# Deviations turned by a small product, and another order of the last five pairs, in a spectral filter with a softmax-gated feed-forward

## The chip, the cores and the metric

The kernel runs on one core of a Trainium2 chip. The core has a matrix engine (TensorE), a vector engine (VectorE, DVE in the profile), a scalar engine (ScalarE, ACT), a general engine (GpSimd, POOL), and a queue engine that only issues transfers (SyncE, SP). Each has its own instruction stream, carried out in order; semaphores tie the streams together. ScalarE and POOL issue transfers too. Products land in PSUM[...].

The metric is the device time of one execution in microseconds. The kernel before took 1626.26 us, the median of three runs (1624.71 to 1630.68).

## The reference

```python
X = np.fft.rfft(x, axis=1)                     # x: (8, 3136, 256)
Y = X * (filt_r + 1j * filt_i)[None]
x = np.fft.irfft(Y, n=3136, axis=1).reshape(25088, 256)
h = x @ w_in                                   # (25088, 1024)
e = np.exp(h - h.max(-1, keepdims=True))
solu = h * e / (e.sum(-1, keepdims=True) + 1e-9)
mu = solu.mean(-1, keepdims=True)
var = ((solu - mu) ** 2).mean(-1, keepdims=True)
out = ((solu - mu) / np.sqrt(var + 1e-6) * g_ln) @ w_out      # (25088, 256)
```

Everything is float32 (the filters and weights come as given to the kernel). Of the deviations this document speaks of, there is one for each of the 25088 rows: 1/sqrt(var + 1e-6). The kernel folds the mean and g_ln into w_out, so that a row of the result is its row of solu times the folded weights, times that row's deviation.

## The kernel before, in words

**Two halves that run together.** The Fourier filter of the eight batch elements is a sequence of small matrix products with trips through DRAM in between (tiles d1 and d2). Element 0 is filtered in a start-up phase. The others are filtered while the feed-forward works on earlier elements. `PLAN` says at which step each piece of an element's filter runs: its first products (`first_at`, line L269 for elements from 2 on), its spectrum (`spectrum_at`, L301 forward and back), and its way back to rows (`back_at`, L372). The filtered rows lie transposed in the tile `y`, which holds two elements.

**The feed-forward's steps.** The 25088 rows are 196 blocks of 128. Two blocks are a pair for the first product; four blocks are a group. `step(k)` is called for k from 0 to 204 (196 blocks and a lag of 9), and writes out by hand what each engine gets, in this order; there is no planner beyond it. `j` is k // 2. With `hid` (k below 196) the step runs products of x with w_in, and with `proj` it runs products with w_out of a pair p that is four to five pairs behind: an odd step has products 1, 2, 6, 7 of p = j - 4, the even step after it products 5, 3, 4 of the same p.

**Seven products in place of eight.** Both matrix products are done by halves in Winograd's form: four sums of quarters of the left operand (`pair_sums`, `project_sums`, on POOL, line L702), sums of weights made once, and seven half-size products (`product`, L723, 128x512 each; `project`, L844, four times 128x128 each). In PSUM the seven go to two banks for the output product (`o0`, `o1`) and two or three for the first (`m0`, `m1`). Products 1, 6, 5 and 3 of a pair all go to bank 0, on top of each other, and ScalarE takes the value out in between: after product 1, after 6 and after 5 (`keep_out`, L856, a scaled copy by the row's deviation), and after 3. Products 2, 7 and 4 go to bank 1, and VectorE joins each with what ScalarE has kept (`finish_out`, L860). `store_out` (L868) sends the pair's 256 rows to DRAM on SP's queue.

**From solu to the left operand of the second product.** `exponential` (L755, ScalarE), `normalize` (L766 to L771, VectorE), `turn` (L787, a 32x32 block transpose on VectorE into a tile `turn` for the group), `square` (L779, ScalarE: the variance of each row, four columns for a group's four blocks). `regroup(p, i)` (L799) then moves quarters of the turned group into tiles `solu_t` in eight DMAs of 128 KB for a pair, on SP's queue. Each quarter takes rows from all four blocks of the group, so the rows of a pair in the second product are not those of two blocks, and a pair's regrouping can only start when all four blocks of its group have been turned. `project_sums(p, 0)` and `project_sums(p, 1)` make the four sums from these tiles in two places of the pair's even step.

**Deviations.** `deviations` (L806 to L810), in the even step in which a group's first pair is regrouped, computes the 128x4 deviations on POOL and stores them to a DRAM row. `regroup_deviations` (L816), one step later, reads them back in the regrouped order with four DMAs:

```python
rows = rs_rows.pop(g).rearrange("(a p) b -> b p a", p=32)
for b in range(4):
    dma(out=rss[g][32 * b:32 * b + 32, :], in_=rows[b])
```

The DMA queue is SP's, but POOL's for the last group. The tile `rs_t` that they fill is what `keep_out` and `finish_out` scale by. In SP's order an even step has: eight regroupings, the deviations' store, two output stores, then loads for the filter; the odd step has the deviations' four reads.

**The first spectrum fetch of an element** (`fetch`, L291) reads d1, which POOL's stores (L280) have just filled. It is issued on ScalarE's queue, except for a part of element 1. Element 2's first one is issued at the end of step 14.

**The tail.** Steps 196 to 204 have no first products any more: TensorE has only the products of the last pairs, 93 to 97. Pair 97 is regrouped one even step after pair 96, though both belong to group 48.

Of the kernel before, what the change touches and what calls it, by code (L numbers as in the profile page):

```python
# [17 lines left out]
P = 128  # L18
# [76 lines left out]
def kernel(  # L95
# [14 lines left out]
    wi_dram = nc.inline_tensor(wi_host, name="wi_tbl").ap()  # L110
    wb_dram = nc.inline_tensor(wb_host, name="wb_tbl").ap()
    de_dram = nc.inline_tensor(de_host, name="de_tbl").ap()

    def pool(name, bufs, space=None, stack=ctx):
        kw = {} if space is None else {"space": space}
        return stack.enter_context(tc.tile_pool(name=name, bufs=bufs, **kw))
# [67 lines left out]
    class Spectrum:  # L184
# [114 lines left out]
        def product(self, i, out, lhsT, rhs):  # L299
            for v in range(self.units[i][1]):  # L300
                nc.tensor.matmul(out=out[:, v, :], lhsT=lhsT(v), rhs=rhs[:, v, :],  # L301
                                 start=True, stop=True)
# [311 lines left out]
    def psum_pair(name, other):  # L614
# [7 lines left out]
    hpool = pool("hp", 2)  # L622
    wk = pool("wk", 1)
    spool = pool("sp", 1)
    rs_dram = pool("rs_dram", 2, DRAM)
    pools |= {name: pool(name + "1", bufs)
             for name, bufs in (("r", 4), ("diff", 1), ("t2", 1), ("p", 1), ("g", 1))}
    pools["de"] = pool("de1", 2)
    second.pools = pools
    for c, at, n, kind, dims in (  # L630
            (0, 0, 4 * C, "t2", "p (v c) -> p v c"), (0, 4 * C, 4 * C, "f", "p (v k c) -> p v k c"),
# [48 lines left out]
    def load_de(sp, u):  # L680
# [3 lines left out]
                            in_=de_dram[i:i + pairs].rearrange("i p k u q -> p i (k u q)"))  # L684
        return de

    turns, variances, solu_ts, solu_sums, rs_rows, rss, pos, ots = (
        {} for _ in range(8))
    sums, ms, hs, nmaxs, es, solus, squares = {}, {}, {}, {}, {}, {}, {}


# [9 lines left out]
    def sum_of(out, in0, in1, op):  # L701
        nc.gpsimd.tensor_tensor(out=out, in0=in0, in1=in1, op=op)  # L702

    def pair_sums(j):

        s14 = upool.tile([P, 2, P], FP32, name=f"s14_{j}", tag="s14")
        s23 = wk.tile([P, 2, P], FP32, name=f"s23_{j}", tag="s23")
        sums[j] = s1, s2, s3, s4 = s14[:, 0, :], s23[:, 0, :], s23[:, 1, :], s14[:, 1, :]
        a11, a12, a21, a22 = (tokens(2 * j + i, c) for i in range(2) for c in range(KD))
        sum_of(s1, a21, a22, ALU.add)  # L710
        sum_of(s2, s1, a11, ALU.subtract)
        sum_of(s3, a11, a21, ALU.subtract)
        sum_of(s4, a12, s2, ALU.subtract)
# [76 lines left out]
    def regroup(p, i):  # L790


        g, second = divmod(p, 2)
        turned = turns[g].rearrange("p (k q) b i -> p k q (b i)", q=4)
        a = 2 * second + i
        st = upool.tile([P, KF, P], FP32, name=f"solu_t_{p}_{i}", tag=f"solu_t{i}")
        solu_ts[p, i] = st[:, 0:KF // 2, :], st[:, KF // 2:KF, :]
        for q in range(4):
            nc.sync.dma_start(out=st[32 * q:32 * q + 32, :, :],  # L799
                              in_=turned[32 * a:32 * a + 32, :, q, :])  # L800

    def deviations(p, dma):
        g, second = divmod(p, 2)
        if not second:
            rs = small.tile([P, 4], FP32, name=f"rs_{g}", tag="rs", bufs=2)
            nc.gpsimd.tensor_scalar(out=rs, in0=variances.pop(g), scalar1=1.0 / DFF, scalar2=EPS_LN,  # L806
                                    op0=ALU.mult, op1=ALU.add)
            nc.gpsimd.tensor_tensor(out=rs, in0=rs, in1=neg_half, op=ALU.pow)
            rs_rows[g] = rows = rs_dram.tile([P, 4], FP32, name=f"rows_{g}", tag="rows")
            dma(out=rows, in_=rs)  # L810

    def regroup_deviations(g, dma):
        rows = rs_rows.pop(g).rearrange("(a p) b -> b p a", p=32)
        rss[g] = small.tile([P, 4], FP32, name=f"rs_t_{g}", tag="rs_t")
        for b in range(4):
            dma(out=rss[g][32 * b:32 * b + 32, :], in_=rows[b])  # L816

    def project_sums(p, step):

        (a11, a12), (a21, a22) = solu_ts[p, 0], solu_ts[p, 1]  # L820
        if step == 0:
            s1 = upool.tile([P, KF // 2, P], FP32, name=f"u1_{p}", tag="u1")
            sum_of(s1, a21, a22, ALU.add)
            sum_of(a21, a11, a21, ALU.subtract)
            solu_sums[p] = s1, None, a21, None
        else:
            s2 = spool.tile([P, KF // 2, P], FP32, name=f"u2_{p}", tag="u2")
            s4 = spool.tile([P, KF // 2, P], FP32, name=f"u4_{p}", tag="u4")
            s1, _, s3, _ = solu_sums[p]
            sum_of(s2, s1, a11, ALU.subtract)  # L830
            sum_of(s4, a12, s2, ALU.subtract)
            solu_sums[p] = s1, s2, s3, s4

    def project(p, m):

        bank = {1: 0, 6: 0, 5: 0, 3: 0, 2: 1, 7: 1, 4: 1}[m]
        if m in (1, 2):
            pos[p, bank] = ps_o.tile([P, DFF // 2], FP32, name=f"o{m}_{p}", tag=f"o{bank}")[:, 0:P]
        s1, s2, s3, s4 = solu_sums[p]
        lhs = {1: solu_ts[p, 0][0], 2: solu_ts[p, 0][1], 4: solu_ts[p, 1][1], 5: s1, 6: s2, 7: s3,  # L840
               3: s4}[m]
        w = w_out_sb[:, {1: 0, 2: 1, 3: 2, 5: 3, 6: 4, 7: 5, 4: 6}[m]]
        for f in range(KF // 2):
            nc.tensor.matmul(out=pos[p, bank], lhsT=lhs[:, f, :], rhs=w[:, f, :],  # L844
                             start=f == 0 and m in (1, 2, 7), stop=True, skip_group_check=True)

# [5 lines left out]
    def keep_out(p, i, to):  # L854
        rs = out_half(p, i, 0)[1]
        nc.scalar.activation(out=out_half(p, *to)[0], in_=pos[p, 0], func=AFT.Copy, scale=rs)  # L856
# [12 lines left out]
        del ots[p]  # L869

    blocks = NT * B // 2

# [8 lines left out]
    for e in range(1, B):  # L883
# [24 lines left out]
        for i, t in enumerate(spectrum_at):  # L908

            other = e == 1 and i % 2 == 1 and t + 1 < LAG  # L910


            dma = nc.sync.dma_start if e == 1 and t < 8 else nc.scalar.dma_start
            fetches = ahead(t, 2) if e == 1 and t < 8 or e == 2 and i == 0 else spectrum_loads[t - 2]
            fetches.append(lambda sp=sp, i=i, dma=dma: sp.fetch(i, dma))
            ahead(t, 1 if e == 1 and i % 2 == 1 else 2).append(lambda sp=sp, i=i: sp.fetch_filter(i))
            fetches.append(lambda sp=sp, i=i: sp.fetch_de(i))
            early[t].append(lambda sp=sp, i=i, o=other: sp.forward(i, psum_pair(f"pb_{sp.e}_{i}", o)))
            add = (nc.gpsimd if t + 1 < LAG else nc.vector).tensor_tensor
            first_parts[t].append(lambda sp=sp, i=i, add=add: sp.multiply(i, 0, add))  # L920
            (top if t + 1 < LAG else second_parts)[t + 1].append(
                lambda sp=sp, i=i, add=add: sp.multiply(i, 1, add))
            late[t + 1].append(lambda sp=sp, i=i, o=other: sp.inverse(i, psum_pair(f"pc_{sp.e}_{i}", o)))
            stores[t + 2].append(lambda sp=sp, i=i: sp.store(i, nc.gpsimd.dma_start))
# [23 lines left out]
    def step(k):  # L948
# [23 lines left out]
        if not odd:  # L972
# [4 lines left out]
                exponential(k - 2)  # L977
            if proj:
                project(p, 5)
                keep_out(p, 1, (0, 1))  # L980
            if blocks <= k < blocks + 2:
                exponential(k - 2)
            if hid and k > LAG:
# [2 lines left out]
                turn(k - 3)  # L986
            if hid and k > LAG:
                finish(j, k, 0, (k, 0), 1)
            if proj:
                finish_out(p, 1, 1, (0, 1), 1)  # L990
            for job in early[k]:
                job()
# [4 lines left out]
                keep(j, k + 1, 0)  # L997
            if proj:
                project(p, 3)
                keep_out(p, 0, (0, 1))  # L1000
                project(p, 4)
            for job in spectrum_loads[k]:
                job()
            if 0 <= j - 3 < pairs:
                regroup(j - 3, 0)
                regroup(j - 3, 1)
            if j - 3 == pairs - 2:
                deviations(j - 3, nc.gpsimd.dma_start)
            if 0 <= j - 4 < pairs:
                project_sums(j - 4, 1)  # L1010
            if j - 3 == pairs - 2:
                regroup_deviations((j - 3) // 2, nc.gpsimd.dma_start)
            elif 0 <= j - 3 < pairs:
                deviations(j - 3, nc.sync.dma_start)
            if hid:
                product(j, 7)
            if 2 <= k < blocks + 2:
                normalize(k - 2)
            for job in second_parts[k] + middle[k] + first_parts[k]:
                job()  # L1020
            if proj:
                finish_out(p, 1, 0, (1, 0), 1)
                store_out(p)
        else:
# [13 lines left out]
            if hid:  # L1038
                product(j, 3)
                product(j, 4)  # L1040
            if 0 <= j - 3 < pairs:
                if (j - 3) % 2 == 0 and j - 3 < pairs - 2:
                    regroup_deviations((j - 3) // 2, nc.sync.dma_start)
            if proj:
                project(p, 6)
                project(p, 7)
# [20 lines left out]

    with tc.manual_schedule():
        pair_sums(0)
        for load in first_loads:  # L1070
            load()
        for k in range(blocks + LAG):
            step(k)
# [30 lines left out]
```

## Time and profile before

| What | Value |
|---|---|
| Median of three runs | 1626.26 us |
| Profiled execution, its own time | 1619.98 us |
| Its span | 1618.2 us |
| TensorE's mean granted clock | 0.991 |
| TensorE busy (PE) | 1548.8 us, 96% |
| VectorE busy (DVE) | 1302.4 us, 80% |
| POOL busy | 1169.3 us, 72% |
| ScalarE busy (ACT) | 903.4 us, 56% |
| Second products, L844 | 402.1 us and 311.0 us |
| First products, L723 | 396.6 us and 308.0 us |
| DMA packets | 377245, of them 62762 under 512 B |

How to read it: the busy time of an engine is the time in which at least one of its instructions ran. PE is the matmuls, PEld the loads of weights, which run under matmuls. Every f32 product is recorded as two matmuls and two loads, so that four 128x128 products are a piece of eight records. A row of a timeline gives the start in us from the span's start, the duration, the engine and line, the tile written and those read, the shape and how many records were merged; in square brackets, the idle time before it and what ended it. A q after an engine's name (SPq, ACTq) is its queue of issued transfers.

### The profile page before, as it was taken

To read this page: it belongs to the slowest core of one execution; us is meant where nothing else is said; L and a number is where in the kernel's file an instruction comes from. 1 tells how busy PE (TensorE), PEld (TensorE's weight loads), DVE (VectorE), ACT (ScalarE), POOL (GpSimd) and SP (SyncE) were. 2 spreads that over 40 slices of the span, in tenths; PEclk is the share of its full clock that TensorE was granted. 3 is DMA by queue.
4 is the path that set the end of the run, shared out by engine and by line. 5 is a ranking of instruction groups with operands and counts; after the bars stand their busy time and mean duration, and the time that the engine had idled before them with its cause. 6 is when DMAs were issued, how large, how long until landed. Compare 5 with 4: busy or idle time off the path is not lost. (4 is left out here: it accounts for less than half of the span.)

```text
span 1618.2 us, 37006 instructions
## 1 busy us (share of the span) xinstructions
PE 1548.8 (96%) x12710; PEld 1048.2 (65%) x12710; DVE 1302.4 (80%) x2630; ACT 903.4 (56%) x1772; POOL 1169.3 (72%) x1333
## 2 busy tenths in 40 slices
PE   5899899999999999999999999999999999999997
PEld 1363456666766677667766676667676777777776
DVE  1686877998898989997999789897988777777772
ACT  2135555566565655666656655566556566665662
POOL 4446887579777877797688867788666766677775
PEclk8999999999999999999999999999999999999999
DMA  9888878877788778866887668866785454444443
GB/s 268 245 268 249 244 208 229 223 209 196 203 246 231 201 189 243 241 192 167 211 251 200 186 180 229 238 180 169 215 234 151 121 135 122 104 112 105 110 110 102
DMA packets 377245, 312.13 MB, mean 193 GB/s; under 512 B 62762, under 2 KB 342835, under 8 KB 377059
## 3 DMA queue, kind: packets, MB, share of 16 engines
q1 hardware_dynamic: 304340, 168.63, 40.3%
q0 software_dynamic: 34624, 101.68, 20.7%
q10 hardware_dynamic: 38096, 39.46, 8.1%
q8 instruction: 103, 1.69, 0.5%
q14 instruction: 82, 0.67, 0.1%
HBM read 124.86 MB, written 81.50 MB: 128 GB/s over the span
## 5 line engine op out<-in xcount | busy, mean ns | idle before, releaser
L844 PEld LDWEIGHTS o<-w_out_sb,solu_t 128*128 128x128 f32 x3136 | 382.8, 192 | 49.3 <-issue 43.9
L723 PE MATMUL m<-w_in_sb,s 128*128 128x512 f32 x784 | 396.6, 607 | 9.9 <-ACT h L733 9.2
L844 PE MATMUL o<-w_out_sb,solu_t 128*128 128x128 f32 x3136 | 402.1, 276 | 2.9 <-DVE ot L860 2.0
L844 PEld LDWEIGHTS o<-w_out_sb,u 128*128 128x128 f32 x2352 | 307.3, 192 | 144.4 <-issue 109.7
L844 PE MATMUL o<-w_out_sb,u 128*128 128x128 f32 x2352 | 311.0, 275 | 7.4 <-ACT ot L856 4.6
L723 PE MATMUL m<-w_in_sb,y 128*128 128x512 f32 x588 | 308.0, 607 | 4.8 <-DVE h L744 2.9
L771 DVE SCALAR_TENSOR_TENSOR h<-e,rsum,h 128x1024 f32<-128x1024 f32 x196 | 302.1, 1541 | 6.9
L733 ACT COPY h<-m 128x512 f32<-128x512 f32 x294 | 172.9, 588 | 237.0 <-PE m L723 204.2
L702 POOL TENSOR_TENSOR u<-solu_t 128x512 f32<-128x512 f32 x98 | 133.3, 1361 | 219.3 <-DMA solu_t<-turn 134.6
L856 ACT ACTIVATE ot<-o,rs_t 128x128 f32<-128x128 f32 x392 | 143.6, 366 | 258.3 <-PE o L844 241.2
L779 ACT ACTIVATE h<-h,nmu 128x1024 f32<-128x1024 f32 x196 | 224.9, 1148 | 53.2 <-DVE turn L787 43.0
L747 DVE CUSTOM_DVE_ANT_0 h<-m,h 128x512 f32<-128x512 f32 x196 | 134.1, 684 | 140.3 <-ACT h L733 102.6
L787 DVE STREAM_TRANSPOSE turn<-h 128x1024 f32<-128x1024 f32 x196 | 243.2, 1241 | 3.2
L755 ACT ACTIVATE e<-h,nmax 128x1024 f32<-128x1024 f32 x196 | 225.1, 1149 | 8.8 <-DVE h L771 8.4
L702 POOL TENSOR_TENSOR u<-solu_t,u 128x512 f32<-128x512 f32 x98 | 149.0, 1520 | 93.4 <-PE o L844 89.2
L723 PEld LDWEIGHTS m<-w_in_sb,s 128*128 128x128 f32 x784 | 128.6, 191 | 98.3 <-issue 85.0
L860 DVE SCALAR_TENSOR_TENSOR ot<-o,rs_t,ot 128x128 f32<-128x128 f32 x294 | 102.0, 347 | 77.0 <-ACT ot L856 60.6
L723 PEld LDWEIGHTS m<-w_in_sb,y 128*128 128x128 f32 x588 | 96.3, 191 | 102.1 <-issue 52.9
L702 POOL TENSOR_TENSOR u<-u,solu_t 128x512 f32<-128x512 f32 x98 | 161.6, 1649 | 0.9
L702 POOL TENSOR_TENSOR solu_t<-solu_t,solu_t 128x512 f32<-128x512 f32 x98 | 153.4, 1565 | 7.7
L702 POOL TENSOR_TENSOR s<-y 128x128 f32<-128x128 f32 x196 | 95.6, 488 | 0.5
L372 PEld LDWEIGHTS py<-wb_t,t 50*64 50x64 f32 x3584 | 57.6, 134 | 42.9 <-issue 22.5
(116 smaller groups left out, 1965.4 us busy)
## 6 DMA issues: line engine op xcount, KB each, us to landing
solu_t<-turn SPq DMA_DIRECT2D x784, 128.0 KB
out_dram<-ot SPq DMA_DIRECT2D x196, 128.0 KB
t<-d POOLq DMA_DIRECT2D x112, 200.0 KB, 6.0
d<-x POOLq DMA_DIRECT2D x100, 200.0 KB, 5.1
f<-f_dram POOLq DMA_DIRECT2D x39, 512.0 KB, 7.2
d<-g POOLq DMA_DIRECT2D x39, 512.0 KB, 4.8
t<-d ACTq DMA_DIRECT2D x37, 512.0 KB
x<-in_x_dram SPq DMA_DIRECT2D x112, 98.0 KB
```

The source lines that it names most:

```text
L372: nc.tensor.matmul(out=views[g][64 * h:64 * h + 64, cb, i, :], lhsT=t4[rows, i, c0:c0 + 64], rhs=wb_t[rows, 0:N1], start=True, stop=True)
L702: nc.gpsimd.tensor_tensor(out=out, in0=in0, in1=in1, op=op)
L723: nc.tensor.matmul(out=ms[j, bank], lhsT=lhsT, rhs=w_in_sb[:, w, :], start=m in (1, 2, 7), stop=True, skip_group_check=True)
L733: nc.scalar.copy(out=h_half(k, i), in_=ms[j, 0])
L747: nc.vector.tensor_tensor_reduce(out=h_half(k, i), in0=ms[j, bank], in1=h_half(*kept), scale=1.0, scalar=sofar, op0=ALU.add, op1=ALU.min, ...
L755: nc.scalar.activation(out=e, in_=hs[k], func=AFT.Exp, bias=nmaxs.pop(k)[:, 1:2], scale=-1.0, accum_out=esum)
L771: nc.vector.scalar_tensor_tensor(out=solu, in0=e, scalar=rsum, in1=solu, op0=ALU.mult, op1=ALU.mult, accum_out=nmu)
L779: nc.scalar.activation(out=solu, in_=solu, func=AFT.Square, bias=nmu, scale=-float(DFF), accum_out=variances[g][:, i:i + 1])
L787: nc.vector.transpose(out=turns[g][:, :, i, :], in_=solus[k].rearrange("p (f j) -> p f j", j=32))
L844: nc.tensor.matmul(out=pos[p, bank], lhsT=lhs[:, f, :], rhs=w[:, f, :], start=f == 0 and m in (1, 2, 7), stop=True, skip_group_check=True)
L856: nc.scalar.activation(out=out_half(p, *to)[0], in_=pos[p, 0], func=AFT.Copy, scale=rs)
L860: nc.vector.scalar_tensor_tensor(out=ot, in0=pos[p, bank], scalar=rs, in1=out_half(p, *kept)[0], op0=ALU.mult, op1=ALU.add)
```

## The change

**Deviations.** The trip through DRAM goes. A constant tile `turn_t` (128x36, loaded once on POOL's queue) holds a one at column (row modulo 32) in its first 32 columns and a one at column (row // 32) in its last four. POOL multiplies the first 32 columns by each of the group's four deviations into a tile of 128x128 (`wide`), in the same place where the deviations were stored. One even step later than `deviations`, behind product 4, TensorE multiplies that tile (as weights) with the last four columns of `turn_t`, and the 128x4 result is the regrouped deviations. It lands in four free columns of the bank that products 2, 7 and 4 of that step's pair use (`places`), and ScalarE copies it to `rs_t`. For the last group too, everything is done this way.

**Sums.** The first place makes sums 1 and 2, the second sums 3 and 4 (before: 1 and 3, then 2 and 4).

**Last five pairs** (`last`, pairs 93 to 97). Product 3 goes to a bank of its own, `m0`, free by then. After product 5 ScalarE takes bank 0 out twice, once for each half of the rows, and VectorE joins product 3 with the second copy in an instruction more. All joins and the store of such a pair come ahead of that step's other VectorE work. The last pair's regrouping follows that of the pair ahead of it in the same step, into a buffer of another pool.

**One fetch** of element 2, the first of its spectrum, moves from ScalarE's queue to SP's.

```diff
+    rows = np.arange(P)[:, None]
+    turn_dram = nc.inline_tensor(np.concatenate(
+        [rows % 32 == np.arange(32), rows // 32 == np.arange(4)], 1).astype(np.float32),
+        name="turn_tbl").ap()
...
-    def deviations(p, dma):
-        g, second = divmod(p, 2)
-        if not second:
...
-            rs_rows[g] = rows = rs_dram.tile([P, 4], FP32, name=f"rows_{g}", tag="rows")
-            dma(out=rows, in_=rs)
...
+    def deviations(g):
...
+        spreads[g] = wide = spread.tile([P, 4, 32], FP32, name=f"wide_{g}", tag="wide")
+        nc.gpsimd.tensor_tensor(
+            out=wide, in0=turn_t[:, 0:32].rearrange("p (o i) -> p o i", o=1).broadcast_to([P, 4, 32]),
+            in1=rs.rearrange("p (b o) -> p b o", o=1).broadcast_to([P, 4, 32]), op=ALU.mult)
+
+    def regroup_deviations(g, ps):
+
+        nc.tensor.matmul(out=ps, lhsT=spreads.pop(g).rearrange("p b i -> p (b i)"), rhs=turn_t[:, 32:36],
+                         start=True, stop=True)
         rss[g] = small.tile([P, 4], FP32, name=f"rs_t_{g}", tag="rs_t")
-        for b in range(4):
-            dma(out=rss[g][32 * b:32 * b + 32, :], in_=rows[b])
+        nc.scalar.copy(out=rss[g], in_=ps)
...
         if step == 0:
             s1 = upool.tile([P, KF // 2, P], FP32, name=f"u1_{p}", tag="u1")
+            s2 = spool.tile([P, KF // 2, P], FP32, name=f"u2_{p}", tag="u2")
             sum_of(s1, a21, a22, ALU.add)
+            sum_of(s2, s1, a11, ALU.subtract)
+            solu_sums[p] = s1, s2
+        else:
+            s4 = spool.tile([P, KF // 2, P], FP32, name=f"u4_{p}", tag="u4")
+            s1, s2 = solu_sums[p]
             sum_of(a21, a11, a21, ALU.subtract)
...
-        bank = {1: 0, 6: 0, 5: 0, 3: 0, 2: 1, 7: 1, 4: 1}[m]
+        alone = m == 3 and p in last
+        bank = 2 if alone else {1: 0, 6: 0, 5: 0, 3: 0, 2: 1, 7: 1, 4: 1}[m]
+        if alone:
+            pos[p, bank] = ps_m.tile([P, DFF // 2], FP32, name=f"o{m}_{p}", tag="m0")[:, 0:P]
...
+    last = range(blocks // 2 - (LAG + 1) // 2, blocks // 2)
...
-            dma = nc.sync.dma_start if e == 1 and t < 8 else nc.scalar.dma_start
+            dma = nc.sync.dma_start if e == 1 and t < 8 or e == 2 and i == 0 else nc.scalar.dma_start
...
             if proj:
                 project(p, 5)
-                keep_out(p, 1, (0, 1))
+                keep_out(p, 1, (1, 1) if p in last else (0, 1))
+            if p in last:
+                keep_out(p, 0, (0, 1))
+                finish_out(p, 1, 1, (1, 1), 1)
...
+            if j >= 4 and j % 2 == 0 and j - 4 < pairs:
+                regroup_deviations((j - 4) // 2, places.pop(p) if proj else psum("ps_rs")[:, 0, 0:4])
...
-            if 0 <= j - 3 < pairs:
-                regroup(j - 3, 0)
-                regroup(j - 3, 1)
-            if j - 3 == pairs - 2:
-                deviations(j - 3, nc.gpsimd.dma_start)
+            if 0 <= j - 3 < pairs - 1:
+                for n in range(j - 3, pairs if j - 3 == pairs - 2 else j - 2):
+                    regroup(n, 0)
+                    regroup(n, 1)
...
+            if 0 <= j - 3 < pairs and j % 2:
+                deviations((j - 3) // 2)
             if hid:
                 product(j, 7)
+            if p in last:
+                finish_out(p, 0, 1, (0, 1), 2)
+                finish_out(p, 1, 0, (1, 0), 1)
+                store_out(p)
...
-            if 0 <= j - 3 < pairs:
-                if (j - 3) % 2 == 0 and j - 3 < pairs - 2:
-                    regroup_deviations((j - 3) // 2, nc.sync.dma_start)
```

## The prediction

> **What bounds the kernel now.** I read the busy shares first, then what TensorE waited for, then busy time by stretch of the span, and last the timelines of the places where TensorE stood still. The page and its chain:
>
> ```profile
> span 1618.2 us, 37006 instructions
> PE 1548.8 (96%) x12710; PEld 1048.2 (65%) x12710; DVE 1302.4 (80%) x2630; ACT 903.4 (56%) x1772; POOL 1169.3 (72%) x1333
> PE 42%; DMA 4%; DVE 1%; SPq 1%; issue 1%; ACT 0%; POOL 0%; DVEq 0%; POOLq 0%; ACTq 0%
> ```
>
> TensorE has 69.4 us without work in 1618.2; nearly all of the traced chain is its products. Two stretches (columns: PE, PEld, DVE, ACT, POOL, clock, DMA share, GB/s):
>
> ```profile
> 1300.00:1400.00 100.00, 100.00 (x915) 72.89 (x914) 76.21 (x168) 60.13 (x119) 67.32 (x79) 1.00 0.47 121
> 1580.00:1618.00 38.00, 26.42 (x216) 24.67 (x215) 7.98 (x18) 9.22 (x22) 19.97 (x19) 0.99 0.40 104
> ```
>
> In the middle TensorE is the bound: what is added to it is paid in full, and what is taken from other engines is worth only the stalls it ends. From 300 to 1300 these stretches leave 9.1 us idle in all, from 130 to 300 some 18 us, in the tail 11.6 us, half of it after the last product. TensorE's longest waits after the start-up (total, times, longest):
>
> ```profile
> PE m L723 <- ACT h L733: 9.2, 6, 3.4
> PE pa L269 <- POOL x L260: 5.5, 6, 2.6
> PE o L844 <- ACT ot L856: 4.6, 8, 1.0
> PE o L844 <- POOL u L702: 2.8, 2, 1.5
> ```
>
> [...] each f32 product is recorded as two loads and two matmuls, and in the one row where 128-column weights meet a shorter stream (98 columns) the pace is
>
> ```profile
> 91.50 14.43 PE L395 MATMUL py<-wi_t,t 100*128 100x98 f32 x128
> ```
>
> 14.43/128 = 0.113 us, hardly more than the 0.111 us of the 128-column stream (1.78 us for 16). So under a short stream the load sets the pace. [...] 62762 packets are under 512 B, and 49 groups with 512 four-byte elements and 128 rows, counted on two sides, are 62720.
>
> **The change, part by part.**
>
> *Small product, +11.0 us.* It has two 128-column loads and two matmuls of 4 columns. At 0.113 us a pair that is 0.226 us; 49 groups make 11.0 us, all on TensorE. The four columns hide no load: the second load and that of the next product lie bare. Bounds: if one of the loads still found cover, 0.113 us (5.5 us); if the pipeline drained around it, two loads of 0.192 us and a fill of 0.17 us (a product of 8 records lasts 1.06 us but follows at 0.89 us), 0.55 us (27 us). I take 0.226, because products of different tiles and banks follow each other in the trace without a gap. Its operand comes from POOL two steps (some 12 us) earlier, so it should not wait for it.
>
> *Work of POOL and ScalarE, +1.0 us.* The 128x4x32 multiplication is not in the trace; nearest is `s<-y` 128x128 at 0.488 us, so 49 times 23.9 us. POOL's idle time (it waits 134.6 us for regrouped tiles alone) covers it, except early, where TensorE waits for POOL's sums (0.94 us at 173.53, 0.97 at 215.41), each behind a deviation: 0.5 us each. Without cover anywhere it would be 23.9. The ScalarE copy, 0.2 to 0.36 us (accumulator read 0.19, a 128x256 copy 0.356), stands where ScalarE waits for the next product anyway. Behind it are DMA issues of the spectrum and, in the next step, the half that product 3 waits for; 2 us of products lie between. [...]
>
> *DMAs taken away, -2.5 us.* SP loses 240 issues (48 at 0.55, 192 at 0.42 us, near 107 us), POOL five, and with them the waits of SP for the row's landing (31.2 us). SP is not on the path by itself. What TensorE can get back are stalls beside these transfers: 2.36 us at 491.85 (ScalarE's own DMA issue stood still while SP put out the four row reads), 0.58 and 1.02 at 1047 and 1049 (a half waited for `rs_t`), 0.97 at 215.41. That is 4.9; I take half, since transfers of 80% share stay around them.
>
> *First fetch of batch element 2, from ScalarE's queue to SP's, -3.4 us.* ScalarE:
>
> ```profile
> 237.89 0.37 ACT L856 ACTIVATE ot<-o,rs_t 128x128 f32<-128x128 f32 x1
> 243.67 0.38 ACTq L291 DMA_DIRECT2D t<-d  x1
> 244.70 0.58 ACT L733 COPY h<-m 128x512 f32<-128x512 f32 x1 [6.44 <-issue]
> ```
>
> The fetch waits for stores that POOL issues until 239.83. Behind it stands the half that product 3 needs, and TensorE loses 3.36 us at 245.43. On SP it is queued behind two output stores, and ahead of the next row loads and regroupings; the forward product that needs it ran at 255.54, so 252 without the stall. Issued at 244 to 246 it should land by then. If it does not, up to 3 us return; I count the gain whole. Its table load remains with ScalarE, without that wait.
>
> *Order of the sums, 0.* POOL does the same four sums; product 6 now has its operand a sum (1.27 us) sooner, product 7 a sum later. Only the tail has such a wait.
>
> *Tail, -4.6 us.* Now:
>
> ```profile
> 1585.68 3.35 PE L844 MATMUL o<-w_out_sb,solu_t 128*128 128x128 f32 x24 [0.33 <-DVE ot L860]
> 1590.36 1.16 PE L844 MATMUL o<-w_out_sb,u 128*128 128x128 f32 x8 [1.33 <-POOL u L702]
> 1606.92 1.16 PE L844 MATMUL o<-w_out_sb,u 128*128 128x128 f32 x8 [1.52 <-POOL u L702]
> 1611.38 1.06 PE L844 MATMUL o<-w_out_sb,solu_t 128*128 128x128 f32 x8
> 1585.54 5.36 SPq L799 DMA_DIRECT2D solu_t<-turn  x8
> 1592.43 6.88 SPq L799 DMA_DIRECT2D solu_t<-turn  x8
> 1603.04 1.26 POOL L702 TENSOR_TENSOR u<-solu_t 128x512 f32<-128x512 f32 x1 [4.05 <-DMA solu_t<-turn]
> ```
>
> The 31 products from 1574.23 would end at 1602.0 without gaps (31 times 0.89 us and 0.17 us of pipeline), and end at 1612.4: 10.4 us of gaps. Not all go. Product 3 in its own bank no longer waits for the evacuation after product 5 (0.72 us a pair), but product 4 still needs VectorE's join of the first half, so some 0.2 us stays. More binding: the last turn ends at 1585.4, and VectorE and ScalarE bring it no sooner. Both regroupings issue from there: pair 96 to 1590.9, its tiles in by 1593.4, two sums of 1.3 us to 1596.1, product 6 then, the rest of the pair with POOL's third and fourth sums to 1601. Pair 97 issues to 1596.3 and lands near 1600 (3.7 us later, as now), two sums to 1602.6; product 6 at 1603.0, then four more at 0.9 us: end at 1607.8 for 1612.4. The joins and 5.8 us to the end stay. Bounds: nothing (the transfers share what they have) to 10.4.
>
> *Sum:* 11.0 + 1.0 - 2.5 - 3.4 - 4.6 = +1.5 us. The profiled execution's span goes from 1618.2 to 1619.7, and its own time from 1619.98 to 1621.5. The median of the runs, 1626.26, lies 6.3 us above that execution; I carry the difference over: 1627.8.
>
> **The rivals.** *A, slower:* the small product drains the pipeline, 0.55 us each, 27 us: +17.5, about 1644. Place: every second even step, behind product 4. It decides from (8.1 + 9.5)/49 = 0.36 us on. For it: one product alone shows 1.06 us against 0.89. Against it: changes of bank and weights cost nothing visible elsewhere. *B, faster:* timed runs are 6.3 us longer than the profiled one; if that is transfer stalls which leave with the small packets, and all 4.9 us of named stalls go too, the sum is 1.5 - 2.4 - 6.3 = -7.2, and with a tail that closes by 7 us -9.6: 1617 to 1619. Against it: from 1300 to 1570 there is no stall left to end. *C, the tail's gain does not come* because both regroupings share the transfer time: +6.1, 1632, still no change. *D, the moved fetch lands late:* +4.9, 1631.
>
> **How the numbers follow.** 0.5% is 8.1 us, about what a measurement of this kernel can tell from no change. Likeliest case 0.38, C 0.12 and D 0.10, all within it (0.60 less 0.02 for combined misses); A and milder forms of it 0.25; B 0.17 to below the bound. So faster 0.17, same 0.58, slower 0.25. The range reaches down into B to 1617 and up into A to 1640; the likeliest's own is 1621 to 1634.
>
> **What would show it.** Small products as a row with 98 matmuls, each group lengthening the stretch behind product 4 by 0.2 to 0.25 us; from 1300 to 1570 of now TensorE stays full and a period of four blocks (24.5 us) grows by that much. ScalarE without the 6.44 us at 244. No packets under 512 B to speak of. The last TensorE product some 4 to 5 us closer to the end of the last hidden product. The forecast is wrong if the small product's pace is over 0.36 us, or if new waits of TensorE for POOL's spread tile, VectorE or SP's queue appear.

## The result and the profile after

The kernel after took 1627.58 us, the median of 13 runs (1622.91 to 1630.88), beside 1626.26 us for 13 runs of the kernel before. The ratio is 0.9991, with an interval of 0.9972 to 1.0011: no difference. The forecast was 1627.8 us, and "no change" its likeliest case. The total is right, but it came from the wrong terms, as the experiments show: the term for the transfers was too small by 18 us, the moved fetch had the wrong sign, and the tail brought nothing.

The two profiled executions should not be set against each other as wholes. That of before ran in 1619.98 us and that of after in 1629.27 us: 9.3 us apart, where the medians differ by 1.3. So the traces are read here by stretch, and sizes are taken from the timed ratios (1% is 16.3 us).

The page of the kernel after:

```profile
span 1627.3 us, 37027 instructions
PE 1557.7 (96%) x12808; PEld 1060.1 (65%) x12808; DVE 1314.6 (81%) x2635; ACT 911.8 (56%) x1821; POOL 1193.7 (73%) x1378
DMA packets 342555, 311.93 MB, mean 192 GB/s; under 512 B 28058, under 2 KB 308147, under 8 KB 342371
```

TensorE has the 98 matmuls of the small products more, and 69.6 us without work, as before (69.4). The busy shares tell nothing of what happened. Of the packets under 512 B some 34,700 are gone and 28,058 are left, so the prediction was wrong to put all 62,762 down to the deviations. It counted each four-byte piece on two sides; an experiment below, with fewer pieces, shows it counted once.

The quiet middle and the tail (columns: PE, PEld, DVE, ACT, POOL, clock, DMA share, GB/s):

```profile
1300.00:1400.00 100.00, 100.00 (x973) 72.96 (x973) 78.89 (x172) 61.30 (x124) 66.91 (x77) 1.00 0.46 118
1589.00:1627.30 38.30, 24.71 (x194) 23.79 (x194) 7.59 (x19) 7.13 (x19) 16.76 (x15) 0.90 0.32 88
```

The middle is full, as before. The tail, which the change was to close up, has 13.6 us without work for TensorE where before had 11.6 in its last 38 us, and a clock of 0.90 for 0.99.

The small product in that middle (timeline of TensorE; start, duration), first before, then after:

```profile
1406.93 1.06 PE L844 MATMUL o<-w_out_sb,solu_t 128*128 128x128 f32 x8
1407.82 1.88 PE L723 MATMUL m<-w_in_sb,s 128*128 128x512 f32 x4
1409.54 1.72 PE L844 MATMUL o<-w_out_sb,solu_t 128*128 128x128 f32 x14
```

```profile
1411.15 1.06 PE L858 MATMUL o<-w_out_sb,solu_t 128*128 128x128 f32 x8
1412.05 0.28 PE L822 MATMUL o<-turn_t,wide 128*128 128x4 f32 x2
1412.19 1.96 PE L728 MATMUL m<-w_in_sb,s 128*128 128x512 f32 x4
1413.99 1.95 PE L858 MATMUL o<-w_out_sb,solu_t 128*128 128x128 f32 x16
```

From product 4 of the pair (L844, now L858) to the next output product TensorE takes 1413.99 - 1411.15 = 2.84 us. Before it took 1409.54 - 1406.93 = 2.61 us. Here the product is paid in full and not more: 0.23 us.

The first fetch of element 2, now on SP's queue, and what waited for it (timelines of SP and TensorE):

```profile
243.42 0.40 SPq L295 DMA_DIRECT2D t<-d  x1
252.06 0.32 PE L376 MATMUL py<-wb_t,t 50*64 50x49 f32 x4 [1.86 <-DMA t<-d]
253.29 1.35 PE L376 MATMUL py<-wb_t,t 50*64 50x49 f32 x60 [0.91 <-DMA t<-d]
258.51 2.01 PE L305 MATMUL pb<-t,de 64*64 64x256 f32 x16 [3.86 <-DMA t<-d]
```

ScalarE's wait of 6.44 us is gone, but TensorE now waits 3.86 us for the fetched tile itself, and 2.77 us for tiles of the way back in the same stretch. Its busy time from 200 to 250 us rose from 44.07 to 46.83 us, and from 250 to 300 us fell from 48.04 to 42.13 us, at a granted clock of 0.90 for 1.00.

The tail after (SP, ScalarE and TensorE):

```profile
1592.27 10.80 SPq L807 DMA_DIRECT2D solu_t<-turn  x16
1603.17 19.94 SPq L883 DMA_DIRECT2D out_dram<-ot  x8
1608.64 0.37 ACT L871 ACTIVATE ot<-o,rs_t 128x128 f32<-128x128 f32 x1 [9.61 <-DMA out_dram<-ot]
1609.15 2.05 PE L858 MATMUL o<-w_out_sb,u 128*128 128x128 f32 x8 [8.43 <-ACT ot L871]
1610.99 1.80 PE L858 MATMUL o<-w_out_sb,solu_t 128*128 128x128 f32 x8
1621.00 1.16 PE L858 MATMUL o<-w_out_sb,solu_t 128*128 128x128 f32 x8
```

The two pairs are regrouped together, in 16 issues of 10.8 us. The output store of pair 94 stands behind these 16 on SP's queue and starts at 1603.17. There are two output tiles `ot`, taken in turn, so pair 96 needs the one that pair 94 has not yet given back: ScalarE waits 9.61 us for the store, and TensorE 8.43 us for ScalarE. From the last product of x with w_in (the last hidden product) to the last product of all it is 43.2 us, counted between the starts of the last records of the two; before had 40.1.

### The profile page after: what moved, and what is told of

Same layout as the page of the kernel before. It is cut to its first block, busy times and chain, and to the rows that moved or that the text cites. A ratio compares the mean times of both kernels' runs of the same rounds, so it can differ in the third digit from the quotient of the medians.

```text
span 1627.3 us, 37027 instructions
## 1 busy us (share of the span) xinstructions
PE 1557.7 (96%) x12808; PEld 1060.1 (65%) x12808; DVE 1314.6 (81%) x2635; ACT 911.8 (56%) x1821; POOL 1193.7 (73%) x1378
## 2 busy tenths in 40 slices
DMA packets 342555, 311.93 MB, mean 192 GB/s; under 512 B 28058, under 2 KB 308147, under 8 KB 342371
## 4 chain that ended last, share of the span: by engine, by line
PE 72%; DMA 8%; DVE 2%; issue 1%; SPq 1%; POOL 1%; ACT 0%; ACTq 0%; DVEq 0%; POOLq 0%
PE o L858 32%; PE m L728 31%; PE py L376 3%; DMA solu_t<-turn 3%; PE pa L273 2%; PE pb L305 2%; PE pc L305 2%; DMA x<-in_x_dram 2%; SPq L807 1%; DMA de<-de_tbl 1%; DMA t<-d 1%; DMA out_dram<-ot 1%; DMA f<-f_dram 1%; POOL u L707 0%; PE o L822 0%
## 5 line engine op out<-in xcount | busy, mean ns | idle before, releaser
L858 PEld LDWEIGHTS o<-w_out_sb,solu_t 128*128 128x128 f32 x3136 | 382.5, 192 | 49.3 <-issue 43.5
L858 PE MATMUL o<-w_out_sb,solu_t 128*128 128x128 f32 x3136 | 402.2, 276 | 3.1 <-DVE ot L875 2.3
L858 PEld LDWEIGHTS o<-w_out_sb,u 128*128 128x128 f32 x2352 | 307.8, 192 | 145.8 <-issue 116.1
L776 DVE SCALAR_TENSOR_TENSOR h<-e,rsum,h 128x1024 f32<-128x1024 f32 x196 | 318.1, 1623 | 6.9
L858 PE MATMUL o<-w_out_sb,u 128*128 128x128 f32 x2352 | 311.8, 276 | 8.5 <-ACT ot L871 8.4
L707 POOL TENSOR_TENSOR u<-solu_t 128x512 f32<-128x512 f32 x98 | 137.5, 1403 | 174.3 <-DMA solu_t<-turn 111.5
L707 POOL TENSOR_TENSOR u<-u,solu_t 128x512 f32<-128x512 f32 x98 | 153.1, 1562 | 20.3 <-PE o L858 12.7
L707 POOL TENSOR_TENSOR solu_t<-solu_t,solu_t 128x512 f32<-128x512 f32 x98 | 163.5, 1669 | 0.9
```

The lines of the kernel that those rows point to most:

```text
L776: nc.vector.scalar_tensor_tensor(out=solu, in0=e, scalar=rsum, in1=solu, op0=ALU.mult, op1=ALU.mult, accum_out=nmu)
```

## The experiments

Each ratio below sets a kernel against runs of the kernel before that were made beside it, so ratios are compared here, and medians are not.

**One part at a time.** The small product without the rest of the change: old tail, old order of the sums, the fetch on ScalarE.

```diff
-            dma(out=rows, in_=rs)
...
-        for b in range(4):
-            dma(out=rss[g][32 * b:32 * b + 32, :], in_=rows[b])
...
+        nc.gpsimd.tensor_tensor(
+            out=wide, in0=turn_t[:, 0:32]..., in1=rs..., op=ALU.mult)
...
+        nc.tensor.matmul(out=ps, lhsT=spreads.pop(g)..., rhs=turn_t[:, 32:36],
+                         start=True, stop=True)
...
+        nc.scalar.copy(out=rss[g], in_=ps)
```

> The kernel before with the small product for the deviations alone (all 49 groups, the last one too); order of the sums, last five pairs and the first fetch of element 2 as before. By the prediction's sum +11.0 (49 products of 0.226 us) +1.0 (POOL) -2.5 (transfers gone) = +9.5 us, ratio 1.006. If the small product drains the pipeline (0.55 us each): 1.016. If the transfers that it takes away were worth as much as the product costs: 1.000. In the quiet stretch, from 1300 us on, where nothing is left to win, the time of four blocks should grow from 24.52 us by 0.22 to 0.25; the traced changed kernel has 24.9 there, so that 0.15 us more would have to come from the new order of the sums.

Measured: 1617.27 us, ratio 0.9953 (0.9935 to 0.9971), faster by 7.6 us where the prediction's first three terms give +9.5. That pointed at the deviations' part as the first wrong one. (The profiled execution of this kernel, with a span of 1627.5 us, had a granted clock of 0.83 in its first 130 us, where before had 0.92; its span says little.)

The last five pairs without the rest, on the kernel before:

```diff
+    last = range(blocks // 2 - (LAG + 1) // 2, blocks // 2)
...
+            alone = m == 3 and p in last
...
+                for n in range(j - 3, pairs if j - 3 == pairs - 2 else j - 2):
+                    regroup(n, 0)
+                    regroup(n, 1)
```

> The kernel before with the last five pairs' part alone (own bank for product 3, joins ahead, the last pair regrouped with the one ahead); deviations, order of the sums and first fetch as before. By the prediction -4.6 us, ratio 0.997. By what the trace of the changed kernel shows (pair 94's output store stands behind sixteen regroupings on SP's queue, pair 96 needs its buffer, TensorE waits 8.4 us), the tail from the last product of the first kind to the last one of all grows from 40.9 us to some 44, ratio 1.002.

Measured: 1630.46 us, ratio 1.0004 (0.9987 to 1.0022). No gain; last hidden to last product 42.9 us.

**The price of the small product.** The change with the product issued twice:

```diff
-        nc.tensor.matmul(out=ps, lhsT=spreads.pop(g)..., rhs=turn_t[:, 32:36], start=True, stop=True)
+        for lhsT in [spreads.pop(g).rearrange("p b i -> p (b i)")] * 2:
+            nc.tensor.matmul(out=ps, lhsT=lhsT, rhs=turn_t[:, 32:36], start=True, stop=True)
```

> The changed kernel with the small product made twice in a row, into the same four columns. What it adds to the changed kernel's ratio of 0.9991 is the price of 49 small products: 0.0068 for 0.226 us each (ratio 1.006), 0.0166 for 0.55 us (1.016), and next to nothing if it is hidden beside other work (below 1.002). In the quiet stretch four blocks take 0.22 us longer than the changed kernel's 24.9.

Measured: 1637.92 us, ratio 1.0071 (1.0050 to 1.0093). That is 0.0080 over the change, 13 us, or 0.27 us for each of 49, within 0.1. The prediction's 0.226 stands, and rival A's 0.55 falls.

**The price of the trip through DRAM: two runs that failed to measure it.** The small product with the old store and reads kept beside it, the reads into a tile that nobody uses:

```diff
+        nc.sync.dma_start(out=rows, in_=rs)
...
+        unused = small.tile([P, 4], FP32, name=f"unused_{g}", tag="unused")
+        for b in range(4):
+            nc.sync.dma_start(out=unused[32 * b:32 * b + 32, :], in_=rows[b])
```

> As dev_alone, and the old trip of the deviations through DRAM is still made (the store of the row and its four reads on SP's queue, in their old places), into a tile that nobody reads. The difference to dev_alone is what the transfers alone cost. By the prediction 2.5 us (ratio 1.007 to 1.0075 here against 1.006); if the transfers are the larger part of the story, 8 us or more (1.006 here against 1.000 or 1.001).

Measured: 1658.18 us, ratio 1.0189 (1.0164 to 1.0214), much more than either case.

The kernel before without the trip; what it leaves out is the turning of the deviations into regrouped order:

```diff
-            rs = small.tile([P, 4], FP32, name=f"rs_{g}", tag="rs", bufs=2)
+            rs = small.tile([P, 4], FP32, name=f"rs_{g}", tag="rs")
...
-            dma(out=rows, in_=rs)
+            rss[g] = rs
...
-        rss[g] = small.tile([P, 4], FP32, name=f"rs_t_{g}", tag="rs_t")
-        for b in range(4):
-            dma(out=rss[g][32 * b:32 * b + 32, :], in_=rows[b])
```

> The kernel before with nothing in place of the trip: the deviations are used as POOL leaves them, not turned, so the regrouping of the deviations is the part left out. It measures the trip's whole price by itself, and, against dev_alone (ratio 0.995), the whole price of what replaces it. Theory now: the small product costs its 11 us, and the trip cost some 18 us, so ratio 0.988 to 0.990. Rival: the product is mostly hidden and the trip cost only the 8 us seen, ratio 0.995.

Measured: 1633.03 us, ratio 1.0028 (1.0008 to 1.0048): slower than before with work taken away. Every theory so far fell with it. A hint stood in the stretch of 1300 to 1400: DMA share 0.56 at 123 GB/s, where before has 0.47 at 121. The packets themselves took longer. Both kernels had also changed the size of a small pool of SBUF that is allocated early, so every later tile had moved.

**Addresses.** The kernel before with nothing changed but two more buffers of a 16-byte tile:

```diff
-            rs = small.tile([P, 4], FP32, name=f"rs_{g}", tag="rs", bufs=2)
+            rs = small.tile([P, 4], FP32, name=f"rs_{g}", tag="rs")
```

> The kernel before with nothing but two more buffers of rs: 32 bytes a partition more in the small pool, so that every later tile in SBUF stands 32 bytes further. No instruction, transfer or wait is added; the only wait that could change is that for a free rs, which never shows. Theory (addresses set the time of the packets, which made the run without the trip and the run with the kept trip slow): DMA share of the quiet stretch 1300 to 1400 about 0.53 at the same 121 GB/s, where before has 0.47, ratio 1.008 to 1.02. Rival (addresses don't matter): 1.000 within 0.002, share 0.47.

Measured: 1664.49 us, ratio 1.0242 (1.0210 to 1.0275). The shift is 64 bytes, not 32, since each buffer takes 32. Its quiet stretch, with a DMA share of 0.54 at 128 GB/s:

```profile
1300.00:1400.00 100.00, 99.56 (x852) 71.93 (x851) 75.82 (x170) 60.25 (x120) 71.45 (x83) 1.00 0.54 128
```

Its main queue on the page (packets, MB, share of 16 engines over the span), then the same line of before:

```profile
q1 hardware_dynamic: 304340, 168.63, 43.5%
```

```profile
q1 hardware_dynamic: 304340, 168.63, 40.3%
```

The same packets and bytes took 0.435 x 16 x 1673.9 = 11,650 us of engine time for 0.403 x 16 x 1618.2 = 10,434: 11.7% more. POOL's wait for regrouped tiles went from 134.6 to 224.1 us. In the allocation of the compiled program the first tile of `turn` starts at byte 97,792 of a partition in before; here it starts at 97,856, in the kernel without the trip at 97,728, and in the one with the kept trip at 97,920. `solu_t`, `ot` and the filter's tiles moved with it: 64 bytes up, 64 down and 128 up. Measured against the kernel that does the same work with its tiles where before has them, packet time on this queue grew by 11.7%, 18.7% and 9.5%. The runs show that the addresses are the cause, but not by the length of the move alone. The packet records of the same traces show which transfer pays. The regroupings move pieces of 512 bytes, and all packets of that size on this queue are theirs; their median is 32 ns in the three kernels with unmoved tiles, and 35, 41 and 35 ns in the moved ones. The medians for 1,024 and 2,048 bytes stay at 46 and 84 ns. Whether the reading or the writing end pays is not shown, since both tiles moved, and neither is why.

**The price of the trip, with addresses kept.** The kernel before without the trip, again with the deviations left unturned, but with every buffer in place:

```diff
-            nc.gpsimd.tensor_tensor(out=rs, in0=rs, in1=neg_half, op=ALU.pow)
-            rs_rows[g] = rows = rs_dram.tile([P, 4], FP32, name=f"rows_{g}", tag="rows")
-            dma(out=rows, in_=rs)
+            rss[g] = small.tile([P, 4], FP32, name=f"rs_t_{g}", tag="rs_t")
+            nc.gpsimd.tensor_tensor(out=rss[g], in0=rs, in1=neg_half, op=ALU.pow)
```

> The kernel before without the trip of the deviations through DRAM: POOL writes the deviations straight into rs_t, unturned (the turning is the part left out), and both tile groups keep their buffers, so that no later tile changes its address; this is what the earlier run without the trip did not keep. Theory (the trip costs TensorE's path about 18 us, since the small product alone came out 7.6 us faster while it adds 11 to 13 us): ratio 0.986 to 0.991, idle TensorE time from 300 to 1200 well under the 9 us of before. Rival (the trip was hidden, and the gain of the small product alone comes from elsewhere, the placement of waits): 0.996 to 1.001, or slower as in the earlier run (1.003).

Measured: 1604.90 us, ratio 0.9876 (0.9848 to 0.9905). And the small product with the kept trip, its unused tile in a pool behind all others:

```diff
-        unused = small.tile([P, 4], FP32, name=f"unused_{g}", tag="unused")
+        unused = spread.tile([P, 4], FP32, name=f"unused_{g}", tag="unused")
```

> The small product alone, with the old trip kept beside it as before, its rows read into a tile that nobody uses; this tile is now allocated behind all the others, so that no address changes (the earlier run with the kept trip had moved them). Theory (address made that run slow; the trip itself costs about 18 us): ratio 1.006 to 1.014, against 0.9953 without the trip and 1.0189 in the earlier run. Rival 1 (the trip itself is what costs): 1.0189 again. Rival 2 (the trip is hidden): 0.996 to 1.000.

Measured: 1636.58 us, ratio 1.0076 (1.0044 to 1.0109). The trip is worth 0.0124 one way (20.2 us) and 1.0076 - 0.9953 = 0.0123 the other (20.0 us), each within 5 to 6 us. TensorE from 300 to 1200, first without the trip, then with product and kept trip:

```profile
300.00:1200.00 900.00, 896.92 (x8078) 617.77 (x8078) 796.91 (x1589) 544.71 (x1078) 696.68 (x804) 1.00 0.76 212
```

```profile
300.00:1200.00 900.00, 887.50 (x7916) 609.72 (x7915) 774.85 (x1539) 533.95 (x1076) 685.29 (x809) 1.00 0.75 206
```

3.1 us idle against 12.5. The other traces agree. Of the kernels with addresses as before, four have the trip (before, the last five pairs alone, this one, and the reads of whole rows below) and 8.8 to 13.7 us idle there; the seven without it have 2.1 to 5.5. What a stall of the second kernel looks like (timelines of SP, ScalarE, TensorE):

```profile
486.04 3.96 SPq L835 DMA_DIRECT2D unused<-rows  x4
490.20 8.21 SPq L809 DMA_DIRECT2D solu_t<-turn  x8
491.94 0.38 ACTq L295 DMA_DIRECT2D t<-d  x1
493.11 1.59 ACTq L690 DMA_DIRECT2D de<-de_tbl  x1
494.74 0.58 ACT L740 COPY h<-m 128x512 f32<-128x512 f32 x1 [5.90 <-issue]
495.47 2.05 PE L730 MATMUL m<-w_in_sb,s 128*128 128x512 f32 x2 [3.22 <-ACT h L740]
```

ScalarE is held by its own DMA issues, while SP has put four tiny reads ahead of its eight regroupings; behind them stands the half that product 3 needs. Nobody reads these rows, so it is not a wait for data. Over the kernel ScalarE's copies of that half wait 15.0 us for their engine's issues here, in three stalls over 3 us. The other three of the four have one or two such stalls, and the seven without the trip have none. What holds an issue of ScalarE back while SP issues is not in the profile. TensorE's wait for the half is 11.2 us here and 3.4 us without the trip. And this stall costs more than its length: the product after the gap of 3.22 us (two records) takes 2.05 us, where it takes 1.02 elsewhere, and the granted clock is 0.50 for 3.41 us from 495.0 on. The trace of before has the same at 245.43, where the product after a gap of 3.36 us takes 2.04 us and the clock is 0.50 for 3.41 us from 245.3 on; after its gap of 2.36 us at 491.85 the clock stays at 1.00. By these figures one such stretch is worth 1.7 us, as an estimate (half of 3.41); from 300 to 1570 there are two here and none in the kernel without the trip. So this pair of traces accounts for 9.4 us of idle time and 3.4 us of slow clock, of the 20 us that the trip costs; where the rest is lost stays open.

Are the small pieces to blame, or the transfers as such? The kernel before with the rows read back in the stored order (the turning is left out), in pieces of 16 bytes in place of 4:

```diff
-        rows = rs_rows.pop(g).rearrange("(a p) b -> b p a", p=32)
+        rows = rs_rows.pop(g).rearrange("(b p) a -> b p a", p=32)
```

> The kernel before with the same five transfers a group on SP's queue, in the same places and with the same bytes, but the four reads take whole rows of 16 bytes (128 pieces a group instead of 512 of four bytes); the order of the deviations is thereby left unturned. If the many small pieces are what the trip cost, most of no_trip's gain is here too, ratio 0.989 to 0.993. If it is SP's time for five issues and its waits, ratio 0.999 to 1.000.

Measured: 1626.48 us, ratio 0.9985 (0.9968 to 1.0002). Packets under 512 B fell from 62,762 to 44,330, which is 128 for 512 in each of the 48 groups read on SP's queue, and the time hardly moved. It is the five transfers in their place on the queue that cost, not their pieces.

**The fetch.** The change with element 2's first fetch back on ScalarE:

```diff
-            dma = nc.sync.dma_start if e == 1 and t < 8 or e == 2 and i == 0 else nc.scalar.dma_start
+            dma = nc.sync.dma_start if e == 1 and t < 8 else nc.scalar.dma_start
```

> The changed kernel with the first fetch of element 2 on ScalarE's queue as before. The traced changed kernel waits 6.6 us near 255 for this tile or what stands behind it, where the kernel before lost 3.4 us behind it on ScalarE. If the place of the fetch is what that stage loses, the ratio falls by 0.002 to 0.997; if late transfers there are the stage's own lot, it stays at 0.999 (with 3.4 us more, 1.001).

Measured: 1622.73 us, ratio 0.9963 (0.9944 to 0.9981), 4.6 us less than the change, give or take 4.5; by the times alone this is hardly clear of nothing. The fetch and the copy behind it (ScalarE):

```profile
237.51 0.38 ACTq L295 DMA_DIRECT2D t<-d  x1
238.55 0.59 ACT L738 COPY h<-m 128x512 f32<-128x512 f32 x1 [2.26 <-PE m L728]
```

Without the trip the stall that the move was to end is not there: the fetch goes out at 237.51, 6 us earlier than on SP, and ScalarE's copy waits for TensorE only. The forward product starts at 251.26 with no wait for it. The other traces say the same. In the four with the trip ScalarE's copy stands 5.4 to 8.2 us at this place behind the fetch; in the four without the trip and with the fetch on ScalarE it does not wait for an issue at all. From the last of POOL's stores that the fetch waits for to the fetch's own issue it is 3.7 to 5.2 us in these eight, and 7.3 to 8.5 us in the three kernels with the fetch on SP, where regroupings and two output stores stand ahead of it. In these three TensorE is busy for 42.1 to 43.9 us from 250 to 300, in the other eight for 46.5 to 48.3.

**The tail.** The change with output tiles of their own for pairs 96 and 97, in memory that the filter no longer uses:

```diff
+            if p in last[3:]:
+                ots[p] = pools["p"].tile([P, 2, C], FP32, name=f"ot_{p}", tag=("pr", "pi")[p - last[3]])
+            else:
                 ots[p] = wk2.tile([P, 2, C], FP32, name=f"ot_{p}", tag="ot")
```

> The changed kernel with output buffers of their own for pairs 96 and 97 (of a pool that is idle in the tail), so that pair 96 does not wait for the store of pair 94; the queue order stays. If that wait is what the tail lost, from the last first product to the last product it takes 36 to 39 us instead of 43.2, and the ratio falls from 0.999 to 0.994 to 0.997. If the regrouped tiles set the tail anyway, the wait of 8.4 us turns into one for the sums of pair 96 and the ratio stays at 0.999.

Measured: 1620.33 us, ratio 0.9946 (0.9925 to 0.9967), 7.3 us less than the change. The same place in its tail:

```profile
1598.70 2.03 PE L858 MATMUL o<-w_out_sb,solu_t 128*128 128x128 f32 x16
1602.21 1.16 PE L858 MATMUL o<-w_out_sb,u 128*128 128x128 f32 x8 [1.48 <-POOL u L707]
1613.15 1.16 PE L858 MATMUL o<-w_out_sb,solu_t 128*128 128x128 f32 x8
```

The 8.43 us have become 1.48, for POOL's second sum. From the last hidden to the last product it is now 35.7 us: 4.4 less than before, where the prediction had worked out 4.6. Not all of it need be the tail's: the small product alone has 38.8 us in its trace.

**The best of it together.** Small product, last five pairs, own output tiles; order of the sums and the fetch as before. Its edit is those of the small product alone, of the last five pairs and of the output tiles.

> The small product and the last five pairs, with the output tiles of pairs 96 and 97 in memory of their own so that neither waits for the store of an earlier pair, the order of the sums and the queue of element 2's first fetch as before. Theory (parts add): 0.9953 for the product, 0.0045 less for the tail that no longer waits: 0.991 within 0.002, time from the last hidden product to the last product 35 to 36 us. Rival (the changed order of the sums is worth something by itself): 0.994 to 0.996, as the whole change with own output tiles had.

Measured: 1616.59 us, ratio 0.9942 (0.9923 to 0.9960), faster than both kernels, but not faster than the small product alone (0.9953) by more than the intervals. The 0.991 of the theory was missed, and the ratio lies in the range of the rival; that the parts add is not shown. Its tail is 37.4 us, 1.7 more than with the new order of the sums. So that order seems to be worth something in the tail. From 1400 us on the traces speak against it: with the small product four blocks take 24.76 to 24.81 us in the three kernels with the old order, and 24.85 to 24.93 in the three with the new one (mean of the last six full groups, by the starts of their first products).

## Why the prediction was right, and where it was wrong

The ratios give each term of the sum a measured value, each within 4 to 6 us. They follow from one another (no trip 0.9876, product added 0.9953, last pairs and sums added 0.9963, fetch moved 0.9991), so that their sum is no test; the kept trip, the doubled product and the own output tiles are independent ones.

| Term | Predicted, us | Measured, us |
|---|---|---|
| Small product and the work of POOL and ScalarE | +11.0 + 1.0 | +12.5; doubled +13.0 |
| DMAs taken away | -2.5 | -20.2; kept beside it -20.0 |
| Fetch of element 2 moved | -3.4 | +4.6 |
| Order of the sums and tail | 0 - 4.6 | +1.6; tail alone +0.7 |
| Sum | +1.5 | -1.5 |

**Small product: right.** 0.23 us in the trace, 0.27 us by doubling. In the row of 98 columns that the prediction read, the loads follow one another without a gap too, 127 in 14.26 us or 0.112 us each, and with 4 columns the pace is still 0.23/2 = 0.115 us. POOL's multiplication took 0.399 us at the median where 0.488 was assumed, and ScalarE's copy 0.16; in the trace no matmul waits for either. The period of four blocks grew from 24.52 to 24.89 us (149.34 us from 1412.05 to 1561.39 in six periods), 0.14 more than the product. With the product and the old order of the sums it is 24.76 to 24.81, so that much of this 0.14 goes with the new order, which the prediction put at 0. VectorE's normalizing row goes the same way: its mean is 1518 to 1585 ns in the seven kernels with the old order, with or without the product, and 1623 to 1639 in the four with the new. That it is the cause was not tried.

**DMAs taken away: the step that failed most.** The prediction saw the right kind of stall, ScalarE's issue held while SP puts out the four row reads, and then summed only the 4.9 us that one profiled execution named, and took half "since transfers of 80% share stay around them". That execution was a quick one, with 8.8 us idle from 300 to 1200 where the other three traces with the trip have 11.6 to 13.7, and the prediction carried its 6.3 us below the median over as if they could not be these stalls; its rival B said they could, at up to -8.7 us. The 0.97 us at 215.41 stands in two of its terms, as a wait for POOL that may grow and as a stall that may go. Neither the prediction nor rival B counted the stretches of 3.41 us at a granted clock of 0.50 behind the gaps of 3.22 and 3.36 us, at some 1.7 us each. These items do not reach 20 us; the rest was not found. Rival B's mechanism was right in kind and too small, but not by way of the small packets, which cost next to nothing: four times fewer in the reads changed the time by 0.15%, less than the interval.

**Fetch: wrong sign, rival D.** The prediction took away ScalarE's 6.44 us and said that on SP the transfer "should land by then". It was issued at 243.42, no later than the 244 to 246 that the prediction gave, and still came too late, 3.86 us of TensorE's time: the product that needs it ran 15.1 us after the issue (13.0 and 15.8 in the other two kernels with the fetch on SP), where the prediction allowed 6 to 8. No line of its own gave that duration; on ScalarE's queue before, issued at 243.67, the product had followed after 11.9 us, not waiting. The other half of the error is that two terms claimed one stall: with the trip gone it had gone as well.

**Tail: mechanism right, one queue overlooked.** The schedule of the two regroupings and the 4.6 us came out once the output tiles were free (4.4 in the trace, 7.3 in the timed ratio against the change). But the step moved eight regroupings ahead of pair 94's store on SP, and the prediction did not ask who waits for that store. With two `ot` tiles it is the pair that the regrouping was to bring forward. The gain fails to come, as in rival C, but not because of shared transfer time.

**The sum** was right because these errors, -17.7, +8.0, +6.2 and +0.5 us, cancel to -3.0. That was luck: a right total is no proof of its terms.

## What to carry to other kernels

A tiny transfer on a busy queue can cost far more than its bytes: here five for each group, 4 KB in all, were worth 20 us, and 9.4 us of TensorE's stalls went with them. Count such stalls over several executions, and add the slow clock behind the long ones (here 3.41 us at 0.50 behind 3.22 us). When an issue is moved on a queue, ask for every instruction now behind it which buffer it frees, and who takes that buffer next. A kernel made to take away one cost must keep all addresses, or it measures something else: here 64 bytes came to 2.4%.

## What the runs showed of the hardware that was not expected

Moving the tiles by 64 bytes, with no instruction added or taken away, cost 2.4% (1.0242, 1.0210 to 1.0275), more than any part of the change was worth. 64 bytes the other way cost 1.5% (1.0028 against 0.9876), 128 bytes up 1.1% (1.0189 against 1.0076). The packets that pay are those of 512 bytes between two tiles: 35 to 41 ns for 32 at the median.

After a gap of 3.22 us the granted clock was 0.50 for 3.41 us, and TensorE took 2.05 us for what takes 1.02; in the changed kernel's tail, after 8.43 us, the first two products took 2.05 and 1.80 us where later ones take 1.06, and the granted clock was 0.50 from 1605.7 to 1612.5.

Five small transfers for each of 49 groups, 2 KB out and 2 KB back, cost 20 us of 1626, and hardly less when the pieces of the reads were four times as long (ratio 0.9985).
